# Stage 0's second matmul taken by halves of the output rows, and the weight work around it re-timed

## The chip, the cores and the metric

The kernel runs on one core of a Trainium2 chip, in one launch. Times are device microseconds (us). TensorE (PE) multiplies, VectorE (DVE) and ScalarE (ACT) work beside it, GpSimd (POOL) and SyncE (SP) mostly issue DMAs. Each engine takes its instructions in program order. PE has two clock levels, 1.2 and 2.4 GHz; the profile gives the granted clock as a share of the upper one.

## The reference

The input of the first block is an attention without softmax over 8 batches of 576 tokens, 8 heads of 64; two feed-forward blocks of 4608 x 512 follow, with d_ff = 2048. All weights come in 64-bit floats.

```
kv  = einsum('bhsd,bhde->...', k, v)          # per head: k^T v
out = q @ kv;  x = out / rms(out) * g_norm    # rows of 64
h1 = x @ w_in;    y = (h1 * sigmoid(1.702 * h1)) @ w_out
h2 = y @ w2_in;   z = (h2 - tanh(h2)) @ w2_out
```

## The kernel before

**Tiling.** Activations are kept transposed. The 4608 tokens run in eight stages of 576 (one batch each), first all eight of block 0 (`l = 0`, `n = 0..7`), then all eight of block 1. A stage is M1 (x @ w_in, eight slices `p` of d_ff, then the activation) followed by M2 (times w_out). Matmuls run in fp16 with each operand split into a high and a low part: three matmuls (`wh xh`, `wh xl`, `wl xh`) of 128 x 128 by 128 x 288 for one product. Most stages use a seven-product scheme for 2 x 2 blocks (L713 `m1`, L846 `m2`: 336 matmuls each). That needs sums of weight blocks. Since these are not ready at the start, M1(0), M2(0) and M1(1) are "plain": eight products, 384 matmuls each (`m1_plain` L954, `m2_plain` L976).

**Weights of block 0.** They are converted on the chip in 32 pieces, 16 of W_in and then 16 of W_out; a piece is (p, h), h being the half of the block's rows or columns. `load_words` (L139) loads it by SP, `words` (L156) turns 64-bit words into f32 (one ACT and three DVE instructions, L161 to L167), POOL stores the f32 form to `wfd` (L204), ACT casts the high part (L208) and DVE subtracts it for the low part (L182). The fp16 halves lie in `wi[p]`; the fourth block of W_out lies in `w3`, a part of tile `st`. Pieces are worked four at a time (`staggered` L185) in buffers cut from `st`, `jt`, `cbk`, `xo1` and `gt`. From `wfd` the sums are made afterwards: `sums_out` (16 pieces: four DVE adds of 128 wide, a cast, a low part, a store to `wod`) and `sums_in` (eight: four adds of 256 wide L176 to L179, two casts L252, two low parts L182, in place in `wi[p]`). M2(1) streams its W_out slabs from `wod` through `st` (L837); M1(2) is the first to use all of `wi[p]`.

**What sets the order.** The program is written out by Python generators, and the order in which they are advanced is the order on each engine. `some(k)` takes k steps of the piece conversion, `adv(k)` runs it until k pieces are done. `add_side(g, a, b)` makes g a side job that gets a steps in each tick of an M1 and b in each tick of an M2 (`tick` L687). Side jobs of stages 0 and 1 are the attention and scaling of the next batch (`both` L1044: matmuls L430, L439, L446; L633 and L358 write the scaled x into `xo`) and the sums; from stage 2 `later` = `conv1` (L214), which converts the weights of block 1.

**Stage 0 and 1.** In M1(0), each of 32 (p, quarter) groups is followed by `some(3)`. M2(0) runs 16 steps (j, q, m), j the half of the tokens: for each, 24 matmuls on all four output rows (mo, d). Its operand (high part ACT L973, low part DVE L974) stands in `JT[k % 3]`, three slots in turn; `operand(k + 3)` follows step k. All W_out pieces are written out by step 6, where `start_sums` (L1120) stores the raw blocks to `wod` and starts `sums`. The sums then run as a side job of M2(0), M1(1) and M2(1), and `drain(dfr)` (L1151) finishes them ahead of M1(2). In M2(1), step i has 12 matmuls; its operand is made by DVE L796 (a difference, for some), ACT L810 and DVE L816, up to five steps ahead, and sums leave PSUM by ACT L864.

Of the kernel before, what the change touches and what calls it, by code (L numbers as in the profile page):

```python
# [83 lines left out]
def body(ctx, tc, att, atp, gn, con, w_in, w_out, w2_in, w2_out, outT):  # L84
# [130 lines left out]
    def conv1():  # L215
# [4 lines left out]
        B = wb.rearrange("p (s f) -> p s f", s=8)  # L220
        load_words(1, *items[0], R[0])
# [46 lines left out]
    def sums():  # L268
# [3 lines left out]
        def feed():  # L272
# [9 lines left out]
            if ready and now[0] >= ready[0][0] + 16:  # L282
                return ready.pop(0)[1]
# [10 lines left out]
    todo_in, todo_out = [], [(p, h) for p in range(NP) for h in range(2)]  # L294
    made, spare, pre = [0, 0], [], []
    pieces, barred, own = [0], [], []

    def convs(items, free):
# [426 lines left out]
    def m1(l, n, hook):  # L725
# [56 lines left out]
        for r, p in seq:  # L782
            step(r, p)
            if r == 7:
                hook(p)
# [166 lines left out]
    plain_banks = [[X[0], X[1], AT[0], AT[1], Y[0], Z[0], Y[1], Z[1]] + six * 4, six * 6]  # L952
# [14 lines left out]
    steps = [(j, q, m) for j in range(2) for q in range(4) for m in range(2)]  # L967

    def operand(k):
        if k < 16:  # L970
            j, q, m = steps[k]
            g, o = GT[q][:, :, 2 * m + j, :], JT[k % 3]
# [4 lines left out]
    def m2_plain(at_step):  # L977
        for k, (j, q, m) in enumerate(steps):
            at_step(k)
            o = JT[k % 3]  # L980
            for mo in range(2):
                s = QW[mo, m]
                for d in range(2):
                    out = ((X, Y) if j == 0 else (Z, X))[mo][d][:, 0:H]
                    for p in range(2):
# [3 lines left out]
                        a, z = k % 8 == 0 and p == 0, k % 8 == 7 and p == 1  # L989
# [3 lines left out]
                    if k % 8 == 7:  # L993
                        if d == 0:
                            b = mscr(T)
                        main(nc.scalar.activation(out=b.ap[:, d * H:(d + 1) * H], in_=out, func=AF.Copy,
                                                  scale=1.0 / (SX * SW[1])))
                        if d == 1:
                            nc.gpsimd.dma_start(
                                out=x2d[2 * mo:2 * mo + 2, :, j * H:(j + 1) * H].rearrange("d p f -> p d f"),  # L1000
                                in_=b.ap[:, 0:T].rearrange("p (d f) -> p d f", d=2))
                            b.free()
            operand(k + 3)
            tick(1)
# [8 lines left out]
    first, words_in = convs([(kind, p, h) for kind in range(2) for p in range(NP) for h in range(2)], places)  # L1013
# [11 lines left out]
    def some(k):  # L1025
        for _ in range(k):
            next(first, None)

# [90 lines left out]

    def start_sums():  # L1120
        for p in range(NP):
            for h in range(2):
                nc.sync.dma_start(out=wod[0][0:3, :, p, h].rearrange("r q t f -> q r t f"), in_=wi[p][:, h, 4:7])
        for p in range(0, NP, 4):
            nc.sync.dma_start(out=wod[0][3, :, p:p + 4], in_=w3[:, p:p + 4])
        stp.extend(k4(stf, 2))
        own.extend(k4(cbk, 3))
        spare.extend(own + stp + late)
        dfr.append(add_side(sums(), 2.4, 3.4))
# [6 lines left out]
    for l in range(2):  # L1136
        for n in range(NS):
# [31 lines left out]
            if (l, n) == (0, 0):  # L1169
# [114 lines left out]
```

## Time and profile before

| | us |
|---|---|
| median of 3 runs (1481.63 to 1485.8) | 1484.47 |
| the profiled execution | 1483.97 |
| its span, first to last instruction | 1482.2 |
| PE busy | 1431.7 (97%) |
| DVE busy | 1144.5 (77%) |
| ACT busy | 879.5 (59%) |
| POOL busy | 168.9 (11%) |

Busy shares are means over stages with different limits. In the trace M1(0) runs from 33.2 to 94.5 us, M2(0) to 147.1, M1(1) to 207.4, M2(1) to 265.1; the other fourteen stages follow. A row of grouped instructions reads: line, engine, operation, written <- read tiles, shapes, count | busy us, mean ns of one | idle us before them and what ended it. A row of waits reads: engine, tile, line that waited <- engine, tile, line waited for: us in total, times, longest.

### The profile page before, as it was taken

Reading aid. Unit: us, or ns where it says so; the run is one execution under the profiler, and the core shown is the slowest. Engines: PE = TensorE matmul, PEld = TensorE weight load, DVE = VectorE, ACT = ScalarE, POOL = GpSimd, SP = SyncE. Lnnn points to the kernel's source line nnn. Section 1 sums busy time; section 2 is a strip of 40 time slices with the busy share of each in tenths; the row PEclk is TensorE's granted clock in tenths of the full one; section 3 lists DMA queues with packets and bytes.
Section 4 is the critical chain, followed back from the end, with each engine's and each line's share of the span. In section 5 each row is a group of like instructions: output and inputs, shape, how many; then the busy total and the mean of one; then the engine's idle time right before and its main releaser. Section 6 shows DMA issues by size and latency. Waiting matters only on the chain.

```text
span 1482.2 us, 30104 instructions
## 1 busy us (share of the span) xinstructions
PE 1431.7 (97%) x11922; PEld 1109.9 (75%) x11922; DVE 1144.5 (77%) x2210; ACT 879.5 (59%) x1918; POOL 168.9 (11%) x262
## 2 busy tenths in 40 slices
PE   7989987999999999999999999999999999999999
PEld 5767665677677777767777777777777777777777
DVE  4996669496795977959799877868777787878485
ACT  5774564565765658657585655656464655555463
POOL 1321010120111212122011100000000000000000
PEclk9999999999999999999999999999999999999999
DMA  8897875458266483664598434250706142331504
GB/s 310 295 355 230 266 253 177 133 158 302 95 231 222 151 309 96 230 220 146 194 320 282 127 127 145 89 167 30 235 11 198 63 151 98 109 124 60 173 15 160
DMA packets 104893, 261.45 MB, mean 176 GB/s; under 512 B 11344, under 2 KB 50384, under 8 KB 104752
## 3 DMA queue, kind: packets, MB, share of 16 engines
q1 hardware_dynamic: 82304, 174.34, 35.5%
q0 software_dynamic: 22448, 85.20, 17.3%
q8 instruction: 93, 1.52, 0.4%
q14 instruction: 48, 0.39, 0.1%
HBM read 208.13 MB, written 51.36 MB: 175 GB/s over the span
## 4 chain that ended last, share of the span: by engine, by line
PE 60%; DVE 17%; DMA 9%; issue 8%; ACT 5%; POOL 1%; SPq 0%; DVEq 0%; ACTq 0%; POOLq 0%
PE X L735 6%; PE X L737 5%; PE X L736 5%; PE X L919 5%; PE X L921 5%; PE X L920 5%; DVE jt L816 4%; PE Z L735 3%; DMA x2d<-mscratch 3%; PE Z L736 3%; PE Z L737 3%; DVE gt L796 2%; PE Y L919 2%; PE Y L921 2%; PE Y L920 2%
## 5 line engine op out<-in xcount | busy, mean ns | idle before, releaser
L810 ACT ACTIVATE jt<-gt 128x576 f16<-128x576 f32 x420 | 284.8, 682 | 174.9 <-PE Y L921 40.9
L816 DVE SCALAR_TENSOR_TENSOR jt<-gt,jt 128x576 f16<-128x576 f32 x420 | 312.0, 754 | 74.3 <-ACT jt L810 73.1
L919 PE MATMUL X<-jt,st 128*128 128x288 f16 x960 | 275.8, 287 | 6.4 <-ACT mscratch L864 6.3
L920 PE MATMUL X<-jt,st 128*128 128x288 f16 x960 | 275.8, 287 | 1.5 <-DVE jt L816 1.5
L921 PE MATMUL X<-jt,st 128*128 128x288 f16 x960 | 275.6, 287 | 0.0
L735 PE MATMUL X<-xo,wi 128*128 128x288 f16 x896 | 257.0, 287 | 6.9 <-ACT mscratch L768 6.2
L737 PE MATMUL X<-xo,wi 128*128 128x288 f16 x896 | 256.8, 287 | 0.0
L736 PE MATMUL X<-xo,wi 128*128 128x288 f16 x896 | 256.8, 287 | 0.0
L920 PEld LDWEIGHTS <-st 128*128 128x128 f16 x1680 | 164.9, 98 | 55.2 <-issue 13.8
L921 PEld LDWEIGHTS <-st 128*128 128x128 f16 x1680 | 164.9, 98 | 47.1 <-issue 5.2
L919 PEld LDWEIGHTS <-st 128*128 128x128 f16 x1680 | 164.8, 98 | 45.7 <-DMA st<-wod 3.7
L735 PEld LDWEIGHTS <-wi 128*128 128x128 f16 x1568 | 153.5, 98 | 52.6 <-issue 13.4
L736 PEld LDWEIGHTS <-wi 128*128 128x128 f16 x1568 | 153.6, 98 | 47.9 <-issue 9.7
L737 PEld LDWEIGHTS <-wi 128*128 128x128 f16 x1568 | 153.6, 98 | 39.1
L768 ACT COPY mscratch<-X 128x288 f32<-128x288 f32 x336 | 133.4, 398 | 76.4 <-PE X L737 68.4
L796 DVE TENSOR_TENSOR gt<-gt 128x576 f32<-128x576 f32 x240 | 176.3, 751 | 1.5 <-ACT gt L742 1.2
L773 DVE TENSOR_TENSOR mscratch<-Z,mscratch 128x288 f32<-128x288 f32 x224 | 101.8, 454 | 60.6 <-ACT mscratch L768 30.8
L919 PE MATMUL Y<-jt,st 128*128 128x288 f16 x480 | 137.6, 287 | 5.4 <-ACT jt L810 3.7
L920 PE MATMUL Y<-jt,st 128*128 128x288 f16 x480 | 137.6, 287 | 2.6 <-DVE jt L816 2.6
L921 PE MATMUL Y<-jt,st 128*128 128x288 f16 x480 | 137.6, 287 | 0.0
L735 PE MATMUL Z<-xo,wi 128*128 128x288 f16 x448 | 128.4, 287 | 0.0
L736 PE MATMUL Z<-xo,wi 128*128 128x288 f16 x448 | 128.3, 286 | 0.0
(248 smaller groups left out, 2488.5 us busy)
## 6 DMA issues: line engine op xcount, KB each, us to landing
st<-wod SPq DMA_DIRECT2D x210, 512.0 KB, 4.6
xo<-atp POOLq DMA_DIRECT2D x20, 640.0 KB, 8.0
scratch<-x2d SPq DMA_DIRECT2D x32, 288.0 KB, 5.1
cbk<-w_in POOLq DMA_DIRECT2D x32, 256.0 KB, 3.4
cbk<-w_out POOLq DMA_DIRECT2D x32, 256.0 KB, 3.9
scratch<-atp POOLq DMA_DIRECT2D x14, 576.0 KB, 7.0
scratch<-rd POOLq DMA_DIRECT2D x28, 288.0 KB, 7.2
x2d<-mscratch SPq DMA_DIRECT2D x28, 288.0 KB, 7.2
```

The costliest lines, as they stand in the source:

```text
L735: nc.tensor.matmul(out=out, lhsT=wh, rhs=xh, start=fresh and kt == 0, stop=False, skip_group_check=k)
L736: nc.tensor.matmul(out=out, lhsT=wh, rhs=xl, start=False, stop=False, skip_group_check=k)
L737: nc.tensor.matmul(out=out, lhsT=wl, rhs=xh, start=False, stop=kt == 1, skip_group_check=k)
L768: main(nc.scalar.copy(out=b.ap, in_=x))
L773: main(nc.vector.tensor_tensor(out=b.ap, in0=add[0], in1=b.ap, op=ALU.add))
L796: tt = lambda o, a, b: main(nc.vector.tensor_tensor(out=G[:, :, o, :], in0=G[:, :, a, :], in1=G[:, :, b, :], op=ALU.subtract))
L810: main(nc.scalar.activation(out=j[:, :, 0, :], in_=GT[STEPS2[i][1]][:, :, QD[STEPS2[i][0]], :], func=AF.Copy, scale=SX))
L816: main(nc.vector.scalar_tensor_tensor(out=j[:, :, 1, :], in0=GT[STEPS2[i][1]][:, :, QD[STEPS2[i][0]], :], scalar=SX, in1=j[:, :, 0, :], op ...
L919: nc.tensor.matmul(out=out, lhsT=wh, rhs=xh, start=a, stop=False, skip_group_check=k)
L920: nc.tensor.matmul(out=out, lhsT=wh, rhs=xl, start=False, stop=False, skip_group_check=k)
L921: nc.tensor.matmul(out=out, lhsT=wl, rhs=xh, start=False, stop=z, skip_group_check=k)
```

## The change

1. W_out's pieces are converted all for h = 0 first, then for h = 1. M1(0) takes 2.4 conversion steps for each group where it took 3, and M2(0) takes 1.2 a step in its first half and 2.0 later.
2. M2(0) runs over d first, the half h of the output rows: 16 steps (q, j, m) of 12 matmuls for d = 0 and the same 16 for d = 1. All 16 operands are made in the first pass and kept: 0 to 2 in `JT`, operand k in the place of the activation that operand k - 3 was made from, so no operand waits for PE to free a slot.
3. Raw blocks go to `wod` by halves at steps 16 and 24 (`raw_out`). The sums start at step 16 with two buffers and get five more at step 24.
4. During M2(1) no `sums_in` is started that isn't under way (`hold`); the last two are made in M1(2), each before its slice p (`upto`), and `conv1` starts once they are done.
5. M1(1) begins in banks Y0 and Y1 in place of X0 and X1.

```diff
@@ conv1
+        while made[0] < NP:
+            yield
@@ sums: feed
-            if ready and now[0] >= ready[0][0] + 16:
+            if ready and now[0] >= ready[0][0] + 16 and not (hold and ready[0][1][2] == 0):
-    todo_in, todo_out = [], [(p, h) for p in range(NP) for h in range(2)]
+    todo_in, todo_out = [], [(p, h) for h in range(2) for p in range(NP)]
@@ m1
         for r, p in seq:
+            if n == 2 and l == 0:
+                upto(p + 1)
             step(r, p)
@@
-    plain_banks = [[X[0], X[1], AT[0], AT[1], Y[0], Z[0], Y[1], Z[1]] + six * 4, six * 6]
+    plain_banks = [[X[0], X[1], AT[0], AT[1], Y[0], Z[0], Y[1], Z[1]] + six * 4,
+                   [Y[0], Y[1]] + [Z[0], Z[1], Y[0], Y[1], X[0], X[1]] * 5]
-    steps = [(j, q, m) for j in range(2) for q in range(4) for m in range(2)]
+    steps = [(q, j, m) for q in range(4) for j in range(2) for m in range(2)]
+    def place(k):
+        if k < 3:
+            return JT[k]
+        q, j, m = steps[k - 3]
+        return GT[q][:, :, 2 * m + j, :].bitcast(F16).rearrange("p a (t f) -> p a t f", t=2)
@@ m2_plain
-        for k, (j, q, m) in enumerate(steps):
-            at_step(k)
-            o = JT[k % 3]
-            for mo in range(2):
-                s = QW[mo, m]
-                for d in range(2):
-                    out = ((X, Y) if j == 0 else (Z, X))[mo][d][:, 0:H]
+        for d in range(2):
+            acc = ((X, Y), (Z, X))[d]
+            for k, (q, j, m) in enumerate(steps):
+                at_step(16 * d + k)
+                o = place(k)
+                for mo in range(2):
+                    s = QW[mo, m]
+                    out = acc[j][mo][:, 0:H]
...
-            operand(k + 3)
-            tick(1)
+                if d == 0:
+                    operand(k + 3)
+                if k % 2:
+                    tick(1)
@@ stage 0
-                    if k < 8 and k % 2 == 0:
-                        adv(min(32, 20 + 2 * k))
-                    if k < 6:
-                        some(4)
-                    elif k == 6:
+                    if k == 0:
+                        withdraw(xot)
+                    elif k == 8:
+                        withdraw(jxt)
+                    elif k == 16:
+                        raw_out(0)
+                        start_sums()
+                    elif k == 24:
                         adv(32)
-                        start_sums()
-                m1_plain(0, ahead_of, lambda p: some(3), behind)
+                        raw_out(1)
+                        more_sums()
+                    if k % 4 == 0 and k < 28:
+                        adv(min(32, 18 + k // 2))
+                    pace(1.2 if k < 16 else 2.0 if k < 28 else 0)
+                m1_plain(0, ahead_of, lambda p: pace(2.4), behind)
@@ stage 1 and after
-                rate(dfr[0], 2.4, 0.85)
+                hold.append(1)
+                rate(dfr[0], 0.4, 0.4)
             if (l, n) == (0, 2):
-                drain(dfr)
+                hold.clear()
                 add_side(later, 0.72, 0.0)
+            if (l, n) == (0, 3):
+                rate(later, 0.8, 0.0)
```

How this moves instructions, at three places. First ACT at the end of M1(0), around the last three activations (written to `gt3`); L208 into `wi4` is the cast of a W_out piece, L161 opens the next piece. Before:

```order
L961 ACTIVATE gt3_76<-Z0_86 128x288
L208 CAST wi4_67<-xo1_72 128x3x128
L208 CAST st_78<-xo1_72 128x128
L961 ACTIVATE gt3_76<-Y1_85 128x288
L161 ACTIVATE st_78<-st_78 128x512
L208 CAST wi4_67<-xo1_72 128x3x128
L208 CAST st_78<-xo1_72 128x128
L961 ACTIVATE gt3_76<-Z1_87 128x288
```

And now:

```order
L968 ACTIVATE gt3_76<-Z0_86 128x288
L161 ACTIVATE jt_77<-jt_77 128x512
L968 ACTIVATE gt3_76<-Y1_85 128x288
L208 CAST wi4_67<-st_78 128x3x128
L208 CAST st_78<-st_78 128x128
L968 ACTIVATE gt3_76<-Z1_87 128x288
```

Before, both halves of slice 4 are cast ahead of the last activation (26 pieces); now one half of it, with one half of slices 0 to 3 (21 pieces).

Second DVE in M2(0), operands 6 to 15 before (L974), with the attention's L450, L582 and L583 between them:

```order
L974 SCALAR_TENSOR_TENSOR jt_77<-gt3_76,jt_77 128x2x288
L182 TENSOR_TENSOR wi7_70<-xo1_72,wi7_70 128x3x128
L182 TENSOR_TENSOR st_78<-xo1_72,st_78 128x128
L974 SCALAR_TENSOR_TENSOR jt_77<-gt0_73,jt_77 128x2x288
L450 TENSOR_TENSOR ms_103<-AT_88,ms_103 128x288
L974 SCALAR_TENSOR_TENSOR jt_77<-gt0_73,jt_77 128x2x288
L582 TENSOR_TENSOR scratch_79<-scratch_79,ms_103 128x288
L583 SCALAR_TENSOR_TENSOR scratch_79<-scratch_79 128x288
L974 SCALAR_TENSOR_TENSOR jt_77<-gt1_74,jt_77 128x2x288 x2
L974 SCALAR_TENSOR_TENSOR jt_77<-gt2_75,jt_77 128x2x288 x2
L974 SCALAR_TENSOR_TENSOR jt_77<-gt3_76,jt_77 128x2x288
```

And now, operands 9 to 15 (L988) in the first pass:

```order
L988 SCALAR_TENSOR_TENSOR gt1_74<-gt2_75,gt1_74 128x2x288
L988 SCALAR_TENSOR_TENSOR gt2_75<-gt2_75 128x2x288
L182 TENSOR_TENSOR wi7_70<-cbk_80,wi7_70 128x3x128
L182 TENSOR_TENSOR st_78<-cbk_80,st_78 128x128
L988 SCALAR_TENSOR_TENSOR gt2_75<-gt3_76,gt2_75 128x2x288 x2
L164 TENSOR_SCALAR xo1_72<-xo1_72 128x512
L165 SCALAR_TENSOR_TENSOR xo1_72<-xo1_72 128x512
L167 SCALAR_TENSOR_TENSOR xo1_72<-xo1_72 128x512
L988 SCALAR_TENSOR_TENSOR gt2_75<-gt3_76,gt2_75 128x2x288
L454 TENSOR_TENSOR ms_103<-AT_88,ms_103 128x288
L182 TENSOR_TENSOR wi0_63<-xo1_72,wi0_63 128x3x128
L988 SCALAR_TENSOR_TENSOR gt3_76<-gt3_76 128x2x288
```

Before, the second half of the operands has no piece between them; now pieces lie between the operands, and seven of them come behind operand 15.

Third DVE at the end of M2(1): the last operands (L816, now L822), the sums out of PSUM (L858, now L864) and a `sums_in` (four adds L176 to L179 and the low parts into `wi7`). Before:

```order
L796 TENSOR_TENSOR gt3_76<-gt3_76 128x2x288
L816 SCALAR_TENSOR_TENSOR jt_77<-gt0_73,jt_77 128x2x288
L176 TENSOR_TENSOR cbk_80<-cbk_80 128x2x128
L177 TENSOR_TENSOR cbk_80<-cbk_80 128x2x128
L178 TENSOR_TENSOR cbk_80<-cbk_80 128x2x128
L179 TENSOR_TENSOR cbk_80<-cbk_80 128x2x128
L816 SCALAR_TENSOR_TENSOR jt_77<-gt1_74,jt_77 128x2x288
L816 SCALAR_TENSOR_TENSOR jt_77<-gt2_75,jt_77 128x2x288
L182 TENSOR_TENSOR wi7_70<-cbk_80,wi7_70 128x4x128 x2
L816 SCALAR_TENSOR_TENSOR jt_77<-gt3_76,jt_77 128x2x288
```

And now:

```order
L802 TENSOR_TENSOR gt3_76<-gt3_76 128x2x288
L822 SCALAR_TENSOR_TENSOR jt_77<-gt0_73,jt_77 128x2x288
L822 SCALAR_TENSOR_TENSOR jt_77<-gt1_74,jt_77 128x2x288
L822 SCALAR_TENSOR_TENSOR jt_77<-gt2_75,jt_77 128x2x288
L822 SCALAR_TENSOR_TENSOR jt_77<-gt3_76,jt_77 128x2x288
L864 SCALAR_TENSOR_TENSOR mscratch_81<-Z0_86,mscratch_81 128x288
L864 SCALAR_TENSOR_TENSOR mscratch_81<-Z1_87,mscratch_81 128x288
L176 TENSOR_TENSOR cbk_80<-cbk_80 128x2x128
L177 TENSOR_TENSOR cbk_80<-cbk_80 128x2x128
```

The `sums_in` of slices 6 and 7 have left M2(1), with their casts on ACT; slice 6's now follows M2(1)'s last instruction on DVE.

## Rows read from the trace of the kernel before

**Rows 1.** Stage stretches: length, PE, PEld, DVE, ACT, POOL busy (count), clock, DMA, GB/s
```profile
33.20:94.50 61.30, 55.12 (x469) 41.06 (x469) 59.23 (x110) 45.36 (x102) 17.74 (x27) 0.95 0.93 313
94.50:147.10 52.60, 50.30 (x430) 38.48 (x428) 39.05 (x80) 29.25 (x59) 8.86 (x16) 1.00 0.86 268
147.10:207.40 60.30, 57.54 (x513) 41.67 (x513) 39.41 (x96) 36.38 (x78) 7.97 (x14) 0.94 0.78 242
207.40:265.10 57.70, 45.95 (x338) 34.37 (x336) 49.49 (x85) 24.88 (x46) 1.86 (x4) 0.94 0.67 219
265.10:320.30 55.20, 52.70 (x490) 38.17 (x488) 38.34 (x83) 38.81 (x99) 11.12 (x17) 1.00 0.32 105
359.90:413.00 53.10, 52.03 (x484) 37.63 (x483) 38.98 (x82) 39.35 (x101) 9.01 (x14) 1.00 0.40 144
902.60:945.90 43.30, 43.30 (x356) 34.59 (x354) 33.20 (x73) 27.01 (x66) 0.72 (x1) 1.00 0.18 58
```

**Rows 2.** The chain of waits: the attention's matmul groups in stage 0
```profile
97.62 0.73 PE AT L430 x20
101.40 0.65 PE AT L439 x8
114.67 0.62 PE AT L446 x8
```

**Rows 3.** Shorter stretches, columns as in rows 1
```profile
110.00:134.00 24.00, 24.00 (x201) 18.66 (x199) 11.34 (x22) 11.77 (x22) 6.13 (x10) 1.00 0.74 237
150.00:160.00 10.00, 9.61 (x74) 6.75 (x72) 6.32 (x17) 3.37 (x8) 0.55 (x1) 0.74 0.94 304
248.00:256.00 8.00, 5.84 (x35) 4.08 (x35) 7.90 (x15) 2.75 (x6) 0.00 (x0) 0.79 0.22 70
```

**Rows 4.** Waits of DVE in M2(0) and of PE around M1(1)'s start
```profile
DVE jt L974 <- ACT jt L973: 12.6, 7, 3.1
...
PE X L947 <- ACT mscratch L996: 2.3, 1, 2.3
PE X L947 <- ACT xo L355: 1.8, 1, 1.8
```

**Rows 5.** Waits in M2(1), 207 to 265 us
```profile
ACT wi L252 <- DVE cbk L179: 16.2, 3, 5.9
...
PE X L919 <- ACT mscratch L864: 4.0, 2, 2.6
PE Y L919 <- ACT jt L810: 3.7, 1, 3.7
DVE cbk L176 <- DMA cbk<-wfd: 3.6, 1, 3.6
```

**Rows 6.** Groups of DVE instructions by line and shape, 33 to 265 us
```profile
L182 DVE TENSOR_TENSOR wi<-cbk,wi 128x512 f16<-128x512 f32 x20 | 13.1, 686 | 0.7 <-ACT wi L252 0.7
L974 DVE SCALAR_TENSOR_TENSOR jt<-gt,jt 128x576 f16<-128x576 f32 x16 | 12.1, 754 | 12.6 <-ACT jt L973 12.6
...
L165 DVE SCALAR_TENSOR_TENSOR cbk<-cbk 128x512 uint32<-128x512 uint32 x10 | 6.9, 693 | 0.3
...
L633 DVE TENSOR_TENSOR scratch<-scratch 128x1152 f32<-128x1152 f32 x4 | 5.4, 1351 | 0.0
...
L164 DVE TENSOR_SCALAR cbk<-cbk 128x512 uint32<-128x512 uint32 x10 | 4.3, 426 | 0.4 <-ACT cbk L161 0.4
...
L179 DVE TENSOR_TENSOR cbk<-cbk 128x256 f32<-128x256 f32 x8 | 3.4, 426 | 0.3
...
L182 DVE TENSOR_TENSOR wi<-cbk,wi 128x384 f16<-128x384 f32 x6 | 3.3, 551 | 0.0
...
L182 DVE TENSOR_TENSOR st<-cbk,st 128x128 f16<-128x128 f32 x6 | 1.7, 284 | 0.0
```

**Rows 7.** DMA issues, 60 to 110 us: bytes each, median us to landing
```profile
wod<-wi SPq DMA_DIRECT2D x13, 192.0 KB, 5.1
...
cbk<-w_out SPq DMA_DIRECT2D x4, 256.0 KB, 7.1
```

**Rows 8.** The same, 196 to 213 us
```profile
cbk<-wfd SPq DMA_DIRECT2D x3, 512.0 KB, 8.5
```

More of the change, by code (lines that the diff above doesn't have):

```diff
@@ L292, in sums @@
             yield
-    todo_in, todo_out = [], [(p, h) for p in range(NP) for h in range(2)]
-    made, spare, pre = [0, 0], [], []
+    todo_in, todo_out = [], [(p, h) for h in range(2) for p in range(NP)]
+    made, spare, pre, hold, busy = [0, 0], [], [], [], []
     pieces, barred, own = [0], [], []
@@ L305, in loads @@
                 it = items.pop(0)
+                busy.append(at)
                 load_words(0, *it, at[:, 0:1024])
@@ L314, in ends @@
             pieces[0] += 1
+            busy[:] = [x for x in busy if x is not c[1]]
             if all(c[1] is not e for e in barred):
@@ L988, in m2_plain @@
                         xh, xl = (o[:, p, t, :] for t in range(2))
[L989 removed]
+                        a, z = q + m + p == 0, q + m + p == 5
                         nc.tensor.matmul(out=out, lhsT=wh, rhs=xh, start=a, stop=False, skip_group_check=True)
@@ L992, in m2_plain @@
                         nc.tensor.matmul(out=out, lhsT=wl, rhs=xh, start=False, stop=z, skip_group_check=True)
[L993 to L996, printed above, removed]
-                                                  scale=1.0 / (SX * SW[1])))
[L998 to L1002, printed above, removed]
-            operand(k + 3)
-            tick(1)
+                    if q + m == 4:
+                        if j == 0:
+                            obs[mo] = mscr(T)
+                        ob = obs[mo]
+                        main(nc.scalar.activation(out=ob.ap[:, j * H:(j + 1) * H], in_=out, func=AF.Copy,
+                                                  scale=1.0 / (SX * SW[1])))
+                        if j == 1:
+                            nc.gpsimd.dma_start(out=x2d[2 * mo + d, :, 0:T], in_=ob.ap[:, 0:T])
+                            ob.free()
+                if d == 0:
+                    operand(k + 3)
+                if k % 2:
+                    tick(1)
     jx = jt[:, 3:7].rearrange("p a b c d -> p (a b c d)").bitcast(F32)[:, 0:2048]
@@ L1012, in body @@
     extra, places = [gtf[3][:, 0:2048], gtf[2][:, 0:2048]], []
-    first, words_in = convs([(kind, p, h) for kind in range(2) for p in range(NP) for h in range(2)], places)
+    first, words_in = convs([(0, p, h) for p in range(NP) for h in range(2)] + [(1, p, h) for h in range(2) for p in range(NP)], places)
     def withdraw(those):
@@ L1027, in some, with pace @@
             next(first, None)
+    owed = [0.0]
+    def pace(k):
+        owed[0] += k
+        some(int(owed[0]))
+        owed[0] -= int(owed[0])
     def adv(k):
@@ L1118, in body, with idle, raw_out, more_sums @@
     late = k4(jx, 2)
-    def start_sums():
[L1121 to L1125, printed above, removed]
+    def idle(those):
+        while any(x is y for x in busy for y in those):
+            next(first)
+    def raw_out(h):
+        for p in range(NP):
+            nc.sync.dma_start(out=wod[0][0:3, :, p, h].rearrange("r q t f -> q r t f"), in_=wi[p][:, h, 4:7])
+        for p in range(0, NP, 4):
+            nc.sync.dma_start(out=wod[0][3, :, p:p + 4, h], in_=w3[:, p:p + 4, h])
+    def start_sums():
+        idle(jxt)
+        spare.extend(late)
+        dfr.append(add_side(sums(), 2.7, 2.5))
+    def more_sums():
         stp.extend(k4(stf, 2))
         own.extend(k4(cbk, 3))
-        spare.extend(own + stp + late)
-        dfr.append(add_side(sums(), 2.4, 3.4))
+        spare.extend(own + stp)
     def withdraw_out():
```

11 lines of the change are left out of this document (7 added, 4 removed).

## The prediction

> **What bounds the kernel now.** The page's first part gives PE 97% busy, a mean over unlike stages, so the table of stretches was read next, one stretch for each stage [rows 1]. A late M2 shows what undisturbed matmuls cost: 43.30 us for 356, 0.1216 us each. One batch's attention has 20 groups for heads and 8 each for numerators and squares in a run of stage 0, which over its four feature tiles is a load of 4 x 0.73 + 4 x 0.65 + 2 x 0.62 = 6.8 us on PE [rows 2]. By these prices M1(0) and M2(0) need 768 x 0.1216 + 6.8 = 100.2 us and take 113.9; M1(1) needs 53.5 and takes 60.3; M2(1) needs 40.9 and takes 57.7 [rows 1]. Some 37 us are lost there, and almost nothing in the stages after. All that the change can win lies in 33 to 265 us.
>
> Then each stage's loss was followed to its cause by the busy times, the waits and short stretches. In M1(0) DVE is busy 59.2 of 61.3 us: it is the bound. In M2(0) it turns round: in 110 to 134 us PE is busy throughout and DVE 11.3 of 24 [rows 3], and DVE's low parts of operands wait 12.6 us [rows 4], since a slot of three comes free only when PE has read it. So work that loads DVE in M1(0) and M1(1) could lie here. At M1(1)'s start PE waits 2.3 us for bank X (the last sums leave it by L996) and 1.8 for `xo` [rows 4], and its clock in 150 to 160 us is 0.74 [rows 3]. In M2(1) DVE is busy 49.5 of 57.7 us; ACT stands 16.2 us behind DVE in the casts of `sums_in`, PE then waits 4.0 and 3.7 us for ACT's sums and operands, and DVE itself 3.6 for a load from `wfd` [rows 5]. In 248 to 256 us PE is busy 5.8 of 8 us at a clock of 0.79 [rows 3].
>
> **The change part by part.**
>
> *M1(0).* A W_out piece costs DVE 0.43 + 2 x 0.69 words and 0.55 + 0.28 for the low parts: 2.6 us, with overlap about 2.5 [rows 6]. ACT's order has the casts of 26 pieces ahead of the last activation before and 21 now, so 5 x 2.5 = 12.5 us leave DVE's 59.2. With 46.7 us of work DVE is no longer the bound; PE is: 384 x 0.1216 = 46.7, the attention work that falls here (3 x 0.73 + 2 x 0.65 + 0.62 = 4.1), and what the stage's clock of 0.95 now costs, 5% of 61.3 = 3.1 [rows 1]. That is 53.9; I take 54.3, **-7**. Ends: -10.5 if the clock and early waits go too, 0 if a piece loaded too late holds the stage.
>
> *M2(0), first pass.* PE needs 192 x 0.1216 = 23.4 and 2.7 of attention: 26 us. DVE has 13 operands at 0.75, the words of 4 pieces at 1.81, 4 low parts at 0.83 and 0.45 of scaling: 20.8 us [rows 6]. It fits, with the chain from ACT's high part to DVE's low part hidden as long as operands are made three steps ahead. No operand waits for a free slot any more (12.6 us), but DVE's waits were not on the path, so that by itself is worth nothing. What comes late next is piece 26: its cast stands behind operand 15 on ACT, and the second pass's first matmuls need it, about 1.8 us, one piece's words. With 2 us for waits that I cannot see in the trace, first and second pass take 49.4 + 2 on PE.
>
> *Second pass and M1(1)'s start.* DVE has words of 6 pieces (10.9), 7 low parts (5.8), two of L633 at 1.35, four more scalings taken at L974's 0.75, and, as my allowance, 3.0 of first sums and 0.9 of the root: 26.3 us [rows 6], against PE's 23.4. So DVE sets when `xo` of batch 1 stands: 87.5 + 26.0 + 1.8 + 26.3, and some 1.4 until ACT has written it, is 143. Before, PE got through its waits at 147.1 + 2.3 + 1.8 = 151.2 [rows 4]. The wait for X goes, because Y0 and Y1 are released by the first pass, long before; the one for `xo` stays. M1(0)'s end to M1(1)'s start is 55.5 us, 56.7 before: **-1.2**. Ends: -5.5 (PE alone: 49.4 + 1.8), +12 (below).
>
> *M1(1).* 53.5 us of PE and 3 for clock and waits, as 6% of 60.3 are lost to the clock now [rows 1]: 56.5 us, from 151.2 to 207.4 it took 56.2: **+0.3**. More `sums_out` lie here (14, nine before), each 1.7 us of adds and 0.8 of low part; DVE is busy 39.4 of 60.3 us and takes 12.5 more. That is 52 of 56.5 us: tight. Ends: -3 and +6 (half of the added DVE work on the path).
>
> *M2(1).* Two `sums_in` leave: 8 adds at 0.426 and 4 low parts at 0.686, 6.1 us of DVE, with the casts that ACT waits 16.2 us for. DVE's 49.5 us become 43.4, still above PE's 40.9; with 1.1 for the start the stage takes 44.5: **-13.2**. The load for which DVE waited 3.6 us is issued earlier: SP no longer reaches it behind a store that waits for slice 3's low part, and 512 KB take 8.5 us to land [rows 8]. Ends: -16.8 (PE alone) and -6.1 (the two alone).
>
> *M1(2).* The same 6.1 us of DVE, and four casts, come in, each just ahead of the slice that reads it. DVE is busy 38.3 of 55.2 us here [rows 1], so there is room, but the first one follows M2(1)'s last instruction on DVE, ahead of new M1 work: **+2**, as this stage already takes 2.1 more than a later M1 (55.2 against 53.1). Ends: 0 and +6.1. `conv1` starts later and is spread over the other stages of block 0, where PE is the bound: 0, ends -1 and +2.
>
> *DMAs.* A store of raw blocks takes 5.1 us and a load of W_out 7.1 in 60 to 110 us [rows 7]. The 8 raw stores of each half stand on SP ahead of later loads; the first half now goes out while pieces 27 to 32 are still due. All loads of these pieces but the last two are issued by then. I take 0, ends 0 and +3. The Trainium skill (DMA: Bandwidth & Descriptors, "Issuing engines are not separate DMA queues") says that DMAs interleave on the same 16 engines whoever issues them; if the raw stores stretch the last loads by 3 us, the gain is 16 and not 19. No run here shows these two side by side.
>
> Sum: -7 - 1.2 + 0.3 - 13.2 + 2 = **-19.1** against the profiled execution's 1483.97: 1464.9. The median shown lies 0.5 above that execution, so **1465**.
>
> **Rivals.**
>
> *Half arrives (1473 to 1480).* The words saved in M1(0) come back one stage later: the second pass and M1(1) have DVE at 26.3 of 25 and at 52 of 56.5 us. If M2(0) gives back the 7 us, -13 + 2 is left: 1473; if M1(1) loses up to 6 more, 1479. For it: DVE's total work up to M2(1)'s end falls by 6.1 us only. Against it: 12.6 us of DVE's waiting in M2(0) are gone.
>
> *Everything arrives (1452).* If no wait is left in 33 to 265 us, 37 us go, of which the clock at the program's start and M1(2)'s 2 us come back: about -32. Against it: DVE's load is above PE's in two of the stretches.
>
> *Slower (1489).* First pass, d = 0. A step is now 12 matmuls, 1.46 us, plus attention 0.17: 1.63. If a piece's work on ACT and DVE comes in between and the two work in turn, an operand comes every 0.75 + 0.75 (ACT taken as slow as L974) + a quarter of a piece's 2.6 + an allowance of 0.5 for handing over, 2.66 us, and PE starves 16 steps by 1 us: +16. Each such wait can lower the clock, as in 150 to 160 (0.74) and 248 to 256 (0.79) [rows 3]: 10 x 0.26 and 8 x 0.21 us, so three times 1.7 to 2.6, +5; and `xo` later by 3. That is +24 against -19: 1489. It decides once the waits of the first pass exceed 19 us. Against it: three operands stand ready at the start, and ACT has been idle over a third of M2(0) (29.3 of 52.6). The Trainium skill (TensorE: Matmul & The Clock Gate, "HAM oscillation — how this bites in real kernels") reports a kernel whose short waits put PE to the slow clock at every tile again. By it the 16 waits would be paid at half clock, more than three times; the trace agrees so far as both stretches with waits show a mixed clock.
>
> *No change (1481 to 1487).* M2(1) stays bound by its own work on DVE and the rest cancels out. It needs two terms to fail at once.
>
> **How the numbers follow.** The forecast has 50%, with a range of its own of 1458 to 1473 (M2(1) by -10 to -15, the start by 0 to -10). Half arrives: 22%; everything: 13%; slower: 9%; no change: 6%. A difference of 0.3% (4.5 us) is about what can be told from none here. Faster is then 50 + 22 + 13 = 85%, same 6%, slower 9%. For 8 in 10 the range runs from 1453, the edge of everything arriving, to 1482, which takes in all of half arriving and the beginning of no change.
>
> **What would show it.** After: M1(0) ends near 87.5 us, DVE there busy under 50; no wait of L988 for a slot, and PE without waits over 1 us in the first pass (if not, the slower rival); one wait near 1.8 us for `wi4` or piece 26 at the second pass's start; M1(1) starts at about 143 and waits for `xo`, not for a bank; M2(1) takes 44 to 46 us with ACT's wait in L252 below 5 us; M1(2) takes 57. The forecast is wrong if DVE's load moves along and M1(1) passes 60 us, or if M2(1) keeps waits of PE for operands.

## The result and the profile after

The changed kernel takes 1500.04 us (median of 4, 1497.73 to 1502.34) against 1484.36 for the kernel before (4 runs): a ratio of 1.0104, 95% interval 1.0086 to 1.0121. The forecast was 1465. It came out slower, by 1.0%, and not by the mechanism of the slower rival. The profiled execution has a span of 1496.0 us, 13.8 more than before.

The first reading is again the table of stretches, a row for each stage from its first matmul to that of the next (M1(0), M2(0), M1(1), M2(1), M1(2), M2(2); columns as in [rows 1]; where two stages overlap, the bound is set so that a row has as many matmuls as its row before, within two):

```profile
31.50:86.40 54.90, 53.25 (x469) 39.88 (x469) 49.24 (x87) 40.56 (x88) 13.67 (x22) 0.98 0.87 291
86.40:148.70 62.30, 53.90 (x431) 39.54 (x429) 44.42 (x87) 32.42 (x67) 11.88 (x21) 0.95 0.80 242
148.70:212.50 63.80, 55.97 (x514) 40.60 (x513) 44.25 (x110) 38.50 (x82) 8.14 (x15) 1.00 0.74 241
212.50:272.50 60.00, 46.25 (x336) 34.36 (x336) 46.59 (x78) 22.85 (x42) 0.80 (x2) 0.89 0.72 233
272.50:326.50 54.00, 52.63 (x490) 38.18 (x489) 36.11 (x78) 38.85 (x100) 7.55 (x12) 1.00 0.25 83
326.50:370.10 43.60, 40.83 (x320) 31.68 (x319) 34.54 (x55) 19.82 (x36) 7.51 (x13) 0.96 0.83 274
```

Against [rows 1], and for M2(2) against this row of before,

```profile
320.30:359.90 39.60, 39.06 (x320) 31.04 (x318) 34.00 (x56) 19.78 (x36) 5.92 (x11) 1.00 0.87 279
```

the differences are: M1(0) -6.4, M2(0) +9.7, M1(1) +3.5, M2(1) +2.3, M1(2) -1.2, M2(2) +4.0, the stages after them +3.6; M1(0) began 1.7 earlier. That is the 13.8. So M1(0) gave nearly what was forecast, M2(0) gave back more than that, and M2(1), the largest term of the forecast (-13.2), lost instead of gaining.

**M2(0): one late load.** What PE waits for between 86 and 149 us (engine, tile, line that waited <- what it waited for: us, times, longest):

```profile
PE Z L1006 <- ACT wi L208: 5.4, 1, 5.4
PE Y L1006 <- ACT gt L987: 1.5, 1, 1.5
PE Z L1008 <- DVE wi L182: 1.0, 1, 1.0
```

In the first pass operands come in time up to the last; the 1.5 is for that one, operand 15, whose high part stands on ACT behind the attention's activations and their two table loads (1.28 us each). The loss is in the second pass, a wait for the cast (L208) of the last W_out piece. It costs more than its 5.4 us, since the clock is lower behind it. Six us ahead of the wait and six behind it (columns as in [rows 1]):

```profile
128.00:134.00 6.00, 6.00 (x51) 4.79 (x50) 0.68 (x3) 0.08 (x1) 0.17 (x1) 1.00 1.03 322
140.20:146.20 6.00, 6.00 (x25) 3.54 (x26) 5.15 (x10) 2.18 (x5) 0.19 (x1) 0.50 0.66 188
```

PE, at the lower of its two levels, got through 25 matmuls where it had done 51: some 3 us on top of the wait. The chain of waits leads from the cast back through ACT and a DMA to SP (start, us, what):

```profile
121.66 0.38 SPq L152
...
122.09 1.24 SPq L153
...
123.38 13.50 DMA cbk<-w_out
136.88 0.02 issue
136.90 0.04 ACTq L161
```

Read from below: ACT could open the piece only at 136.9, because its load landed then; the load was issued at 121.7, when a buffer came free. The summary of the DMAs in 122 to 131 us suggests why it took 15 us (queue: packets, MB, share; then issues with KB each and median us to landing):

```profile
q0 software_dynamic: 411, 1.61, 72.4%
q1 hardware_dynamic: 407, 0.64, 28.0%
issues: line engine op xcount, KB each, median us to landing
...
wfd<-cbk POOLq DMA_DIRECT2D x2, 256.0 KB, 12.2
cbk<-w_out SPq DMA_DIRECT2D x1, 256.0 KB, 13.3
```

POOL's queue (q0) moves a burst, in packets of 3.9 KB on average: the next batch's `scratch<-rd` and `scratch<-atp` (1.8 MB, issued from 118.0 to 121.0 us) and, behind them, stores of W_out pieces. SP's queue (q1) has packets of 1.6 KB. Each got the same number of packets, 411 and 407, and so SP 28% of the bytes. The Trainium skill (DMA: Bandwidth & Descriptors, "Queues, rings and completion order") says that a DMA engine takes turns between its queues by whole packets, each of several descriptors. The equal counts agree, as far as a packet of the trace can stand for one of these.

**M2(1): another late load, and queues behind it.** The waits from 212 to 273 us, of ACT, DVE and PE (the 3.1 stands ahead of M2(1)'s first matmul, so it lies in the row of M1(1)):

```profile
ACT wi L254 <- DVE cbk L179: 12.1, 1, 12.1
...
DVE cbk L176 <- DMA cbk<-wfd: 8.9, 1, 8.9
PE X L925 <- ACT gt L968: 8.8, 1, 8.8
PE Y L925 <- ACT gt L968: 3.1, 1, 3.1
```

The chain around the load:

```profile
203.17 0.68 DVE cbk L182
203.85 0.03 DVE cbk L176
203.88 4.36 DMA wod<-cbk
208.24 0.02 issue
208.26 14.94 DMA cbk<-wfd
223.20 0.03 issue
```

And ACT's instructions behind the load:

```profile
225.12 1.14 ACT L254 CAST wi<-cbk 128x512 f16<-128x512 f32 x2 [12.07 <-DVE cbk L179]
226.17 0.40 ACT L968 ACTIVATE gt<-X 128x288 f32<-128x288 f32 x1
```

The last `sums_out` (low part at 203.2) stores its result from the buffer that the sixth `sums_in` loads into; the load goes out when the store has landed, behind four slab loads and beside POOL's loads, and lands at 223.2. DVE's adds wait for it, ACT's cast L254 waits for the adds, and in ACT's queue behind the cast stands the last activation of M1(1), which PE needs. In the kernel before, the last `sums_out` had its low part 22 us earlier:

```profile
181.12 0.69 DVE L182 TENSOR_TENSOR cbk<-cbk 128x512 f16<-128x512 f32 x1 [0.68 <-ACT cbk L263]
```

The wait of ACT in the casts fell from 16.2 [rows 5] to 12.1, but it came as one piece and at the place where PE has nothing else.

### The profile page after: what moved, and what is told of

It is laid out like the page before. It is cut to its first block, busy times and chain, and to the rows that moved or that the text cites. A ratio compares the mean times of both kernels' runs of the same rounds, so it can differ in the third digit from the quotient of the medians.

```text
span 1496.0 us, 30090 instructions
## 1 busy us (share of the span) xinstructions
PE 1431.0 (96%) x11922; PEld 1108.0 (74%) x11922; DVE 1146.4 (77%) x2210; ACT 880.8 (59%) x1918; POOL 166.8 (11%) x262
## 4 chain that ended last, share of the span: by engine, by line
PE 60%; DVE 15%; DMA 6%; ACT 6%; issue 3%; SPq 0%; POOL 0%; ACTq 0%; DVEq 0%; POOLq 0%
PE X L739 6%; PE X L925 6%; PE X L927 6%; PE X L926 6%; PE X L741 6%; PE X L740 6%; DVE jt L822 4%; PE Z L739 3%; DVE gt L802 3%; PE Z L741 3%; PE Z L740 3%; PE Y L925 3%; PE Y L927 3%; PE Y L926 3%; DMA st<-wod 1%
## 5 line engine op out<-in xcount | busy, mean ns | idle before, releaser
L816 ACT ACTIVATE jt<-gt 128x576 f16<-128x576 f32 x420 | 284.4, 682 | 187.4 <-PE Y L927 44.5
L822 DVE SCALAR_TENSOR_TENSOR jt<-gt,jt 128x576 f16<-128x576 f32 x420 | 312.0, 753 | 79.8 <-ACT jt L816 78.7
L926 PEld LDWEIGHTS <-st 128*128 128x128 f16 x1680 | 165.1, 98 | 60.1 <-issue 18.2
L739 PEld LDWEIGHTS <-wi 128*128 128x128 f16 x1568 | 153.3, 98 | 52.2 <-issue 13.4
```

What stands on the lines that cost most here:

```text
L739: nc.tensor.matmul(out=out, lhsT=wh, rhs=xh, start=fresh and kt == 0, stop=False, skip_group_check=k)
L816: main(nc.scalar.activation(out=j[:, :, 0, :], in_=GT[STEPS2[i][1]][:, :, QD[STEPS2[i][0]], :], func=AF.Copy, scale=SX))
L822: main(nc.vector.scalar_tensor_tensor(out=j[:, :, 1, :], in0=GT[STEPS2[i][1]][:, :, QD[STEPS2[i][0]], :], scalar=SX, in1=j[:, :, 0, :], op ...
L926: nc.tensor.matmul(out=out, lhsT=wh, rhs=xl, start=False, stop=False, skip_group_check=k)
```

## The experiments

Ratios are against the kernel before. Names with a_ are variants of the changed kernel, those with b_ of the kernel before.

**The last pieces loaded earlier** (`a_slot`).

```diff
-                    if k == 0:
-                        withdraw(xot)
-                    elif k == 8:
+                    if k == 8:
                         withdraw(jxt)
+                    elif k == 20:
+                        withdraw(xot)
```

> The changed kernel, with the two buffers in xo1 kept for the conversion until step 20 of M2(0) (step 0 in the change): the last two W_out pieces are loaded into them some 5 us earlier, and ahead of the first loads of the sums. Theory (a late load: piece 32's load is issued at 121.7 us behind 512 KB of the sums' loads, shares the DMAs with POOL's burst and lands 15 us later, so PE stands 5.7 us for its cast): the wait of PE for wi in the second pass goes below 1 us, M1(1) starts 5 to 7 us earlier, 1493 to 1496 us against the changed kernel's 1500. Rival (the second pass is bound by DVE's work and xo comes no earlier): PE's wait goes, M1(1) starts within 2 us of 148.7, 1498 to 1501.

1493.38 us, 1.0059 (1.0042 to 1.0076), 6.7 less than the changed kernel. The loads, issued at 108.6 and 111.0, land in 4 to 5 us, in a stretch in which POOL's queue sends little (the DMAs of 108 to 117 us):

```profile
q1 hardware_dynamic: 2705, 1.83, 69.5%
q0 software_dynamic: 85, 0.28, 7.6%
```

PE waits for no cast in the second pass. M2(0) and M1(1):

```profile
88.30:142.60 54.30, 52.15 (x431) 38.97 (x430) 44.24 (x87) 32.28 (x67) 12.05 (x21) 0.97 0.87 265
142.60:206.90 64.30, 55.93 (x514) 40.59 (x512) 44.35 (x110) 38.51 (x82) 8.11 (x15) 1.00 0.77 249
```

M2(0) falls by 8.0 with DVE's work unchanged (44.2 and 44.4): the late load, not DVE's work, was its price, 5.4 us of waiting and the lower clock behind it. Something comes back: in 116 to 120 us the clock is 0.63 here, behind the wait of 1.5 us for operand 15, where it stays at 1.00 in the changed kernel. M1(1) stays long.

**Raw stores later** (`a_raw24`): `raw_out(0)` moved from step 16 to step 24.

> The changed kernel, with the raw blocks of the first half stored at step 24, together with those of the second, in place of step 16. Theory (the late load of piece 32 comes from the sums' loads ahead of it and POOL's burst beside it; the first half's stores have landed by 112 us): PE's wait of 5.7 us in the second pass stays within 1.5 us, 1498 to 1503 us. Rival (the raw stores in SP's queue delay the last loads): the wait goes, 1493 to 1496.

1500.40 us, 1.0097 (1.0080 to 1.0114); PE's wait for the cast is 6.0. The raw stores of the first half are not the cause.

**Sums from step 24** (`a_sums24`): `start_sums()` moved from step 16 to step 24.

> The changed kernel, with the sums started at step 24 of M2(0) in place of 16, so that no load of theirs lies ahead of piece 32's. Theory (queue): piece 32 lands 3 to 6 us earlier, PE's wait for its cast falls from 5.7 to 0 to 2 us; the sums come later by some steps, which M1(1) pays in part: 1495 to 1500 us. Rival (POOL's burst alone delays the load): the wait stays above 4 us, 1499 to 1503.

1499.83 us, 1.0104 (1.0086 to 1.0121). The wait only falls to 4.1: the sums' loads ahead in SP's queue are the smaller part of the delay, against my theory. That POOL's burst is the larger part is inferred from the packet counts; no run moves the burst itself. The gain is lost again: the sums end later (last low part at 208.5 us, 203.2 in the changed kernel) and PE waits 17.1 us for W_out's first slab:

```profile
PE Y L925 <- DMA st<-wod: 17.1, 1, 17.1
PE Z L1006 <- ACT wi L208: 4.1, 1, 4.1
```

**Three sums_in in M1(2)** (`a_hold5`): the flag `hold` is replaced by a count.

```diff
-            if ready and now[0] >= ready[0][0] + 16 and not (hold and ready[0][1][2] == 0):
-                return ready.pop(0)[1]
+            for i, (t, c) in enumerate(ready):
+                if now[0] >= t + 16 and not (c[2] == 0 and begun[0] >= lim[0]):
+                    begun[0] += c[2] == 0
+                    return ready.pop(i)[1]
```

`lim` is 5, and 8 from M1(2) on; the changed kernel has six begun by then.

> The changed kernel, with five sums_in started before M1(2) and three in it (six and two in the change): the sixth, whose load is issued at 208 us and lands at 223, no longer stands at the start of M2(1). Theory (DVE waits 8.9 us for that load, ACT 12.1 for DVE with an activation queued behind, and PE 9.1 for that): these waits go, PE waits under 2 us at the start of M2(1), the stage takes 52 to 55 us in place of 62.8, M1(2) 1 to 3 more, 1490 to 1494 us. Rival (the burst of loads then delays W_out's slabs or the next batch's x instead): a wait for a DMA takes its place, 1497 to 1501.

1490.96 us, 1.0044 (1.0029 to 1.0058), 9.1 less. The wait of 8.8 is gone; one of 3.9 for an operand is left. M2(1):

```profile
214.90:266.50 51.60, 46.00 (x336) 34.65 (x336) 43.72 (x72) 22.05 (x41) 0.53 (x1) 0.90 0.79 266
```

The run takes the sixth `sums_in` out with its work (DVE is busy 43.7 us in M2(1), 46.6 in the changed kernel), so it does not part the late load from the work. `a_slot_nohold`, below, has two more `sums_in` in M2(1) and costs 5 to 6 us more; by that price some 3 of the 9.1 us are the work, an estimate.

**Both** (`a_slot_hold5`).

> Both cures at once on the changed kernel: xo1's two buffers kept until step 20, and five sums_in before M1(2) with three in it. Theory (two separate late loads): the gains of 6.6 and 9 us add up, 1483 to 1486 us, no faster than the kernel before; M1(1) still takes some 61 us and M2(1) some 53, against 56.5 and 44.5 forecast. Rival (one cause, M2(0)'s delay handed on): the second cure adds less than 3 us to either, 1488 to 1491.

1482.96 us, 1.0002 (0.9990 to 1.0013): the gains add up (15.1 us by the ratios; 6.7 and 8.9 singly). Two late loads, the second with its `sums_in`, made the changed kernel slower than before. They don't make up the rest of the way to 1465, 18 us. That lies in M1(1) (62.5 us from its seventh matmul, 56.5 forecast), in M2(1) (50.7, 44.5 forecast) and in the stages from M1(3) to block 1's second (547.6, 541.8 before; counted, as in all that follows, from the 13th matmul of either M1).

**sums_in as before, with the earlier loads** (`a_slot_nohold`): `hold` out, `rate(dfr[0], 2.4, 0.85)` and `drain(dfr)` back.

> The changed kernel with xo1's two buffers kept until step 20, and with the sums_in left as in the kernel before: worked on all through M2(1), finished ahead of M1(2), conv1 started there. Theory (six or eight sums_in in M2(1), the first of them with its late load, hold the stage about alike): M2(1) keeps the wait of 9 us and takes 1 to 6 us more than with the hold, M1(2) a little less, conv1 2 to 5 us less in the later stages: 1491 to 1497 us. Rival (the sums_in of M2(1) were worth the 13.2 us that I forecast): 1502 to 1507.

1498.50 us, 1.0102 (1.0086 to 1.0118). A little above the theory's range. What the change does about `sums_in` is worth 5 to 6 us, not 13: taking two out leaves the one that hurts.

**The same count on the kernel before** (`b_hold5`): `lim` as above, so that all three `sums_in` of M2(1) leave it, where the change takes out two; `upto`; the sums at 0.4 steps a tick in stage 1 as in the changed kernel; and `conv1` from when the sums are done.

> The kernel before, with five sums_in before M1(2) and three in it (all eight before it otherwise), conv1 from when they are done; M2(0), W_out's conversion and the banks as before. Theory (M2(1) was held by its three sums_in, and here the loads of the sums and of W_out's slabs do not come behind late sums_out): M2(1) takes 44 to 50 us in place of 57.7, M1(2) up to 3 more, later stages up to 5 more: 1473 to 1480 us. Rival (the burst of loads at M2(1)'s start holds the stage whatever the sums do): M2(1) above 53 us, 1480 to 1486.

1506.61 us, 1.0157 (1.0142 to 1.0172), a miss in the total. In its own stage the theory holds: M2(1) takes 46.0 us, at full clock.

```profile
210.40:256.40 46.00, 41.53 (x337) 32.68 (x336) 42.58 (x71) 21.60 (x39) 1.81 (x4) 1.00 0.79 271
```

At M1(3) the kernel is 8.7 us ahead of before; from there to the second stage of block 1 it loses 31.6. Waits of PE from 350 to 960 us, this kernel:

```profile
PE Z L926 <- DMA st<-wod: 14.1, 5, 4.3
PE Y L926 <- DMA st<-wod: 5.9, 1, 5.9
PE X L740 <- ACT mscratch L773: 5.4, 8, 2.1
```

W_out's slabs come late; before, PE waits 0.9 us for them in those stages. Which part of this is `conv1`'s, the next runs ask.

**Banks alone** (`b_banks`): the kernel before with item 5.

> The kernel before, with M1(1) begun in banks Y0 and Y1, and nothing else changed. In the kernel before these banks are not those released by the first pass, since M2(0) finishes all output rows together. Theory of the prediction (the wait of 2.3 us for X goes, and the wait for xo stays): M1(1) starts 0 to 2 us earlier, 1482 to 1485 us. Rival (xo's arrival alone decides the start): no difference in M1(1)'s running start, 1484 to 1486.

1483.71 us, 0.9997 (0.9987 to 1.0007). M1(1)'s first matmul starts 2.4 us earlier, its seventh at 149.9 as before: `xo` alone decides, and the wait for X was cover.

**conv1 faster** (`b_hold5_rate`): `b_hold5` with `rate(later, 0.8, 0.0)` from stage 3.

> The kernel before, with five sums_in before M1(2) and three in it, and conv1 at 0.8 steps a tick from stage 3 on (0.72 in the kernel before and in the run without this). Theory (the late conv1 at the old pace is what costs 30 us in the later stages: its loads and stores meet the W_out slabs, for which PE waits 20 us there): the waits for slabs fall below 6 us, the time is 1474 to 1480 us, faster than the kernel before. Rival (conv1's late start costs this by itself): 1495 or more.

1480.28 us, 0.9984 (0.9969 to 0.9998); 26 us come back, PE waits 6.1 for slabs. The pace of the late `conv1` was the cost.

**Four sums_in in M1(2)** (`a_slot_hold4`): `lim` 4.

> The changed kernel with xo1's two buffers kept until step 20, four sums_in before M1(2) and four in it. Theory (the fifth one's casts stand on ACT ahead of M1(1)'s last activations, for which PE waits 3.1 us at the start of M2(1)): this wait goes, M1(1)'s running start to M2(1)'s start falls from 62.5 to 59 to 60 us, M1(2) takes 1 to 3 more: 1480 to 1484 us. Rival (the wait at M1(1)'s end comes from the attention's table loads and from late sums_out): the wait stays above 2 us, 1482 to 1486.

1494.22 us, 1.0084 (1.0066 to 1.0102), a miss. The wait of 3.1 goes, M1(1)'s running start (its seventh matmul, from which on it waits for `xo`) to M2(1) falls to 60.1 us from 62.5; 3.3 appear for an operand in M2(1), and the later stages take 13 us more (560.6 from M1(3) to block 1's second stage, 547.6 in `a_slot_hold5`), which I put down to `conv1`, later still.

**Three steps a group in M1(0)** (`a_best_pace3`): `pace(3.0)` in `a_slot_hold5`.

> The changed kernel with xo1's two buffers kept until step 20, five sums_in before M1(2), and the conversion in M1(0) at three steps a group, as in the kernel before, in place of 2.4. Theory (taking five pieces out of M1(0) gave the 7 us that I forecast): M1(0) takes 59 to 62 us in place of 55, M2(0) loses its wait of 2.5 us for piece 26 and some of the second pass's DVE work: M1(1)'s running start 2 to 5 us later, 1484 to 1488 us. Rival (the time saved in M1(0) is all given back in M2(0)): no difference, 1481 to 1485.

1490.32 us, 1.0047 (1.0033 to 1.0062), above the theory's range. M1(0) is back at 61.3 us, and M2(0) takes 55.6, more than the 54.2 without:

```profile
31.30:92.60 61.30, 55.18 (x469) 41.00 (x469) 59.22 (x110) 45.31 (x102) 17.69 (x27) 0.95 0.93 318
92.60:148.20 55.60, 52.49 (x431) 39.27 (x430) 33.58 (x64) 26.48 (x53) 8.97 (x16) 0.97 0.77 236
```

The spread of W_out's conversion is worth its 7 us, and M2(0) has room for it.

**conv1 faster still** (`a_best_rate9`): 0.9 for 0.8 in `a_slot_hold5`.

> The changed kernel with xo1's two buffers kept until step 20, five sums_in before M1(2), and conv1 at 0.9 steps a tick from stage 3 on in place of 0.8. Theory (a conv1 that starts later costs some 4 us in the stages after, through waits for slabs): M1(3) to the second stage of block 1 takes 543 to 546 us in place of 547.6, 1479 to 1483 us. Rival (those stages are bound by PE and the difference is chance): no difference beyond 1.5 us.

1493.74 us, 1.0073 (1.0054 to 1.0092), a miss the other way: PE now waits 13.4 us for ACT's evictions (L775) in the stages from M1(3) on, 6.3 at 0.8. More of `conv1` in a stage isn't free.

**conv1 at its old times** (`b_fast`, `a_fast`): `b_hold5` and `a_slot_hold5` with the three `sums_in` early in M1(2) (`rate(dfr[0], 2.5, 0.4)`) and `conv1` at 0.72.

> The kernel before, with five sums_in before M1(2) and three in it, and these three made in the first part of that stage (2.5 steps of the sums a tick), so that conv1 reaches 4, 9, 14, 19, 24 and 29 pieces at the starts of stages 3 to 8, as in the kernel before, at its old pace of 0.72. Theory (sums_in moved out of M2(1) are worth some 9 us up to M1(3), and a conv1 at the old times costs nothing): 8 to 10 us ahead at M1(3), and still so at the end: 1473 to 1477 us. Rival (the later stages give a part back even with conv1 at its old times): 1478 to 1483.

> The changed kernel with xo1's two buffers kept until step 20, five sums_in before M1(2), three early in it, and conv1 at its old pace and times (4, 9, 14, 19, 24, 29 pieces at the starts of stages 3 to 8). Theory (two late loads and conv1's shift make up the difference from the kernel before; M2(0) and M1(1) together are worth 0 to 2 us): 1474 to 1479 us. Rival (the later stages' loss has nothing to do with conv1's times): 1481 to 1485.

1482.86 us, 1.0004 (0.9985 to 1.0024), and 1486.13, 1.0025 (1.0008 to 1.0042): the rivals. `b_fast` is 12.2 us ahead at M1(3), and 10.7 of them are gone by block 1's second stage. Some of it is lost by ACT at M1(3)'s start, and in the same way at M1(5)'s.

```profile
347.20 0.41 ACT L871 ACTIVATE mscratch<-X 128x288 f32<-128x288 f32 x1 [0.32 <-PE X L928]
352.83 0.40 ACT L773 COPY mscratch<-X 128x288 f32<-128x288 f32 x1 [5.21 <-DMA x2d<-mscratch]
353.12 0.22 ACT L436 COPY kv<-AT 128x64 f32<-128x64 f32 x1
```

The same eviction before:

```profile
362.06 0.40 ACT L768 COPY mscratch<-X 128x288 f32<-128x288 f32 x1 [0.98 <-DMA x2d<-mscratch]
```

The eviction of bank X waits 5.21 us (0.98 before) until a store has left the scratch that it writes to, and PE waits with it, 3.1 us at either start.

**No adds in sums_out** (`a_noadds`): `a_fast` without the four adds of each `sums_out`.

> As the run before this, with the four adds of each sums_out left out (their results are then the blocks themselves; 64 DVE instructions of 0.28 us, about 18 us of DVE in M2(0)'s second pass and M1(1); casts, low parts, loads and stores stay). Theory (M1(1) takes 4 to 5 us more than before because 14 sums_out lie in it, whose adds hold ACT's casts and so its activations): M1(1)'s running start to M2(1)'s start falls from 62 to 56 to 59 us. Rival (the busy DMAs delay the attention's loads and so M1(1)): 61 to 63 us, with the same waits in the attention's matmuls.

1483.46 us, 0.9999 (0.9986 to 1.0011). M1(1), `a_fast` and then this:

```profile
142.00:206.50 64.50, 55.99 (x515) 40.61 (x514) 44.27 (x110) 38.54 (x82) 8.41 (x15) 1.00 0.76 249
```

```profile
141.00:200.60 59.60, 55.67 (x515) 40.62 (x513) 29.44 (x54) 38.79 (x82) 7.78 (x14) 1.00 0.85 279
```

From its running start 57.8 us instead of 62.7, as by the theory, and 57.5 in the kernel before: the adds of the `sums_out` in M1(1) make it long. DVE is busy only 44 of 64 us there, so it must be by the order in which ACT and DVE take them; the clearest case is PE's wait of 3.1 at the end, 0.7 without the adds.

**conv1 at its old steps** (`b_phase`, `a_phase`): `b_fast` and `a_fast` with two more steps of `conv1` at the start of M1(3). Their `conv1` was two steps behind; a piece takes eight.

```diff
+            if (l, n) == (0, 3):
+                for _ in range(2):
+                    next(later)
```

> As the run with three early sums_in on the kernel before, with two more steps of conv1 at the start of M1(3): from there on conv1 has done 40, 80, 120, ... steps at the starts of the stages, as in the kernel before, and every engine's order is that of the kernel before. Without them it is two steps of eight behind in each stage, with the same count of pieces. Theory (the 10 us that the later stages gave back come from conv1's place within the stages, by waits of ACT's evictions at their starts): M1(3) to the second stage of block 1 takes 541 to 544 us, 1471 to 1475 us in all, faster than the kernel before. Rival (it is the times of stores and loads, not the order): 546 us and more, 1477 to 1483.

> The changed kernel with xo1's buffers kept until step 20, five sums_in before M1(2), three early in it, conv1 at its old pace, and two more steps of conv1 at the start of M1(3), so that its place in the later stages is that of the kernel before. Theory (conv1's place): M1(3) to the second stage of block 1 takes 541 to 544 us in place of 551, 1474 to 1478 us. Rival (times of stores and loads): 546 us and more, 1479 to 1486.

1473.47 us, 0.9925 (0.9907 to 0.9942), and 1478.25, 0.9965 (0.9953 to 0.9977). Both beat the kernel before, by 0.7% and 0.3%, and `b_phase` is the fastest measured. The totals are those of the theory; the stretch itself takes 546.3 and 546.6 us, where the rival had put it: 5 to 6 less than without the two steps, still 4.5 more than before. In `b_phase` PE's wait falls from 3.1 to 0.7 us at M1(3)'s start and from 3.1 to 0.2 at M1(5)'s; in `a_phase` 2.7 of 3.9 us stay at M1(3)'s. So the order explains about half of what the later stages give back in the traces. What the other half is, stays open: the same order of instructions takes 4.5 us more when it starts 13 us earlier.

## Why the prediction was wrong

- *M1(0), -7*: right. 54.9 us against 54.3 forecast; DVE is busy 49.2, and `a_best_pace3` takes the gain away again.
- *First pass*: right. No operand but the last was waited for (1.5 and 0.5 us, for the two parts of operand 15); the slower rival's mechanism did not occur. Piece 26 cost 1.0 us, 1.8 forecast. That rival also let each such wait lower the clock: it stayed at 1.00 from 112 to 134 us, with all these waits in it, and fell to 0.63 in `a_slot` behind the same 1.5 and 0.5.
- *DMAs, "I take 0, ends 0 and +3"*: the step that failed first. "All loads of these pieces but the last two are issued by then" was true, and the last of the two was the one that counted. I priced a load with its landing time in 60 to 110 us, 7.1 us [rows 7], where 15 were due, and asked what the raw stores would do to it, which was nothing (`a_raw24`). That stretch was no quieter, 352 GB/s against 250 in 122 to 131 us; but POOL's queue sent one packet in eight there, and one in two here. What I had not looked for is POOL's burst in the same 20 us. Cost: 8.0 us of M2(0) (`a_slot`).
- *M1(1)'s start, -1.2*: without that load the length comes out: `a_slot` runs from M1(0)'s end to M1(1)'s running start in 56.0 us, 55.5 forecast. The gain does not. My 151.2 for the kernel before adds the wait for X to a first matmul that comes after it (147.1); the seventh matmul was at 149.9, so before took 55.4 and not 56.7. The wait for X was worth nothing (`b_banks`).
- *M1(1), +0.3 with an end at +6*: from its running start 62.0 us (150.5 to 212.5), 56.5 forecast, 57.5 before. The size is near the end that I named, half of 12.5 us of added DVE work on the path, but by luck: DVE got only 4.8 us busier (44.3, 39.4 before). I had counted 9 `sums_out` in M1(1) before, where the trace has 11, and priced their adds at 0.426 us, the time of the wider ones of `sums_in`; they take 0.29. What the runs show is that the adds cost 4.9 us (`a_noadds`), and that 3.1 are one wait at the stage's end, for an activation behind the casts of a `sums_in` (gone in `a_slot_hold4`).
- *M2(1), -13.2*: failed in its premise. The load "is issued earlier", I wrote; it left SP at 208.3, since it waits for the store of the last `sums_out`, which the change itself had made late (203.2 us, 181.1 before). One load of 512 KB took 14.9 us to land, 8.5 in [rows 8]. I counted two `sums_in` out and not the one that stayed at the stage's start with an activation behind it. With that one out too, M2(1) takes 51.6 us (`a_hold5`), with DVE busy 43.7, as forecast: the stage did not follow DVE's busy time, as my sum for it had it. Where the sums end early it takes 46.0 (`b_hold5`), 11.7 less than before with three `sums_in` out, where I had 13.2 for two.
- *M1(2), +2*: it came to -1.2. The room for `sums_in` is there, even for three.
- *conv1, 0 with ends at -1 and +2*: M2(2) and the later stages took 7.6 us more, of which `conv1`'s new pace and place can be a part; in the variants the place alone moved the total by 9.4 (`b_fast` to `b_phase`) and the pace by 26 (`b_hold5` to `b_hold5_rate`). In the changed kernel itself I did not separate it.

The "half arrives" rival had the nearest thought, that the work comes back a stage later, but added it up in DVE's busy time. The delays were in when loads land and in what stands behind a waiting instruction.

## What to carry to other kernels

A moved step brings its loads to another moment of the program: before calling a load hidden, list what the other queues move in the same 20 us, and take its landing time from a stretch in which they send as many packets, not from one that is merely as busy. On an engine that works in order, ask of every instruction that waits for a load what stands behind it; one such wait of 12.1 us at a stage's start cost PE 8.8 us at once, where three of 16.2 together had cost 7.7 [rows 5]. A side job that starts late stands at another place within every stage that follows: give it back its steps (9.4 us from `b_fast` to `b_phase`), not only its average pace.

## What the runs showed of the hardware

Two busy DMA queues shared by packets and not by bytes: 411 packets of 3.9 KB beside 407 of 1.6 KB in 9 us. It was so again in 213 to 223 us, beside the other late load: 343 packets (1.29 MB) and 341 (1.25 MB), where SP's were larger and so got half of the bytes.

A wait of some 3 us of PE can be followed by a lower clock. The two stages of `b_fast` that begin with a wait of 3.1 us run at a mean clock of 0.98, 2% of 97.0 us or 1.9 on top of the wait, and the two after them at 1.00; the low clock stands right behind the wait (0.58 in 353 to 357 us). Two of the four:

```profile
349.30:446.30 97.00, 92.42 (x804) 69.35 (x801) 73.82 (x139) 59.83 (x137) 16.14 (x26) 0.98 0.55 194
446.30:539.40 93.10, 91.18 (x805) 68.72 (x802) 73.79 (x139) 58.93 (x135) 16.13 (x26) 1.00 0.58 200
```

It need not be: behind the 3.06 us at M2(1)'s start the changed kernel ran at 1.00 (212.5 to 217.7 us), and `a_fast`, behind a wait of the same 3.06 us at the same place, at 0.59 (206.5 to 210 us). The waits for operand 15 (1.00 in the changed kernel, 0.63 in `a_slot`) are such a pair too. What makes the difference, these runs do not show.
